# Attention, soft mixture of experts and a softplus layer on one core: q and k in one transfer, w_in in long runs, masks made on the chip

## The chip, the cores and the metric

The kernel runs on one core of one Trainium2 chip. The metric is the time of one execution on the device in microseconds. A second number, the span, is what the hardware profiler records of one execution, from the first to the last thing that it sees; times within the profile count from the start of the span. The core's engines are called PE (TensorE: matmuls and transposes; PEld is its weight load), DVE (VectorE), ACT (ScalarE), POOL (GpSimd) and SP (SyncE, which here only issues transfers). Transfers run on 16 DMA engines that all queues share.

## The reference

Three layers follow one another on 2304 tokens of width 512 (batch 4 x 576 positions; 8 heads of 64). All inputs but w_in and w_out are float32; those two are float64.

```
scores = (q @ k.T) / 8, causal, window of 64;  attn = softmax(scores) @ v     # 4 x 8 x 576 x 64
x      = attn, heads side by side                                            # 2304 x 512
logits = x @ phi                                                             # 2304 x 32 slots
slot_in  = softmax over tokens(logits).T @ x                                 # 32 x 512
slot_out = relu(slot_in[e] @ w1[e]) @ w2[e]      for 8 experts of 4 slots, inner width 1024
x      = softmax over slots(logits) @ slot_out                               # 2304 x 512
out    = softplus(x @ w_in) @ w_out                                          # inner width 2048
```

## The kernel before

**Stage one** (lines 497 to 570) works through 18 tiles of 128 tokens. For a tile, `do_s` multiplies q by the keys of its two blocks of 64 positions (32 small matmuls, L239); `do_t` adds the mask and takes the row maximum on DVE (L250, four operations for each of two halves), `do_m` subtracts the maximum on GpSimd (L257), `do_e` takes the exponential on ACT, `do_pt` transposes on PE with the unit matrix, `do_pv` multiplies by v. The result is normalised, transposed and multiplied by phi; every four tiles a running softmax over tokens is updated. While this goes on, the 32 tiles of w1 (512 KB each) are loaded.

**Stage two** (lines 574 to 749) multiplies the slots by w1 (L594) and w2 (L637). The 32 tiles of w2 are loaded into what stage one and w1 leave free. The first tiles of w_in and w_out are queued before the last two of w2 (lines 732 to 739).

**Stage three** (from line 750) converts w_in and w_out from float64 bit patterns into float32 on DVE (`conv`, L721 to L729, four steps for each half tile), multiplies the slots' output by w_in (`do_wd`, L824, for the first tile), and then computes hidden blocks (`do_h`, L858), softplus on ACT and DVE, and the output products (`do_y`, L887 to L889: three matmuls for each block of 128 x 512, with high and low parts).

**Constants.** One tile `cst_sb` of 128 x 768 floats holds the unit matrix (columns 0 to 127), four masks of 128 columns, of which three are used (128 to 639; the last block is zero), and a selection matrix (640 to 767). It is filled on the host and loaded in one transfer on ACT's queue (L568), behind k of tile 0. A mask has a left and a right half of 64 columns; 0 keeps a score, -8e9 removes it. Mask 1 is for the first tile of a sequence that begins in its upper half, mask 2 for one that begins in the lower half, mask 0 for all others. After stage one, columns 128 to 639 are reused.

**Transfers.** q and k come in tiles of 128 x 512 floats, 2 KB for each partition, v in rows of 2080 bytes. SP issues all of them (k of tile 0 excepted, which ACT issues). There are four buffers each. q of tile t may be loaded when the scores of tile t-4 are done, k when those of t-3 are. A w_in tile is 128 x 4 runs of 1 KB (line 705), a w_out tile 128 runs of 4 KB.

**Order.** Nothing is scheduled at run time. `arrange` simulates the engines with a cost for each step, delays between them and due times, and writes down one order for all engines; each engine then executes its own part of that order and waits at the first instruction whose data isn't there. In stage one, `Q` stands for SP, with costs of 0.67 us for q, k and v and 1.31 us for a w1 tile; `rel` is the earliest start of a step, `FREE_AT` when an engine is free first.

Of the kernel before, what the change touches and what calls it, by code (L numbers as in the profile page):

```python
# [20 lines left out]
FIRST = {0, 9, 18, 27}  # L21
NKB = NQB = NVB = 4
# [15 lines left out]
FREE = dict(E=7.2, A=0.28, D=0.28, P=0.28, Q=0.1)  # L38
FREE_AT = dict(E=3.0, A=4.0, D=3.0, P=3.0, Q=3.6)
L2_END, GOAL, SLACK, NEAR = 7.3, 12.0, 0.65, 0.1  # L40
DELAY = dict(E=0.2, Q=1.0)
LANDS = 2.0
TILE = 4.6
# [5 lines left out]
def arrange(steps, free, ports, tweaks=()):  # L49
# [26 lines left out]
    def make_ready(k):  # L76
        t = steps[k][2]
        for d in steps[k][1]:
            e, end = done[d]
            wait = 0 if e == "Q" and e in steps[k][0] else LANDS if e == "Q" and d[0][0] == "L" else DELAY.get(e, 0.13)  # L80
            t = max(t, end + wait)
        ready[k] = t
# [34 lines left out]
@with_exitstack  # L117
def block_kernel(ctx: ExitStack, tc: tile.TileContext, q, k, v, phi, w1, w2, w_in, w_out, cst, out):
    nc = tc.nc
# [19 lines left out]
    ident = cst_sb[:, 0:128]  # L139
    masks = [cst_sb[:, 128 + 128 * i:256 + 128 * i] for i in range(4)]  # L140
    selr = cst_sb[:, 640:768]
# [50 lines left out]

    kr = sp0.tile([128, NKB, 4, 128], F32, name="kr")
    qb = [sp0.tile([128, 4, 128], F32, name=f"qb{i}") for i in range(NQB)]
    s_acc = sp1.tile([128, DM], F32, name="s_acc")
# [14 lines left out]
    def do_lq(e, t):  # L210
        nc.sync.dma_start(out=qb[t % NQB], in_=q[t])

    def do_lp(e):
        nc.sync.dma_start(out=phi_sb, in_=phi)

    def do_lk(e, t):
        (nc.sync if e == "Q" else nc.scalar).dma_start(out=kr[:, t % NKB], in_=k[t])

# [8 lines left out]
    def do_s(e, t):  # L227
        for a in range(2):
            s_ps[2 * t + a] = bank((2 * t + a) % 3, "s_ps")
        b = t % NKB  # L230
        pb = (t - 1) % NKB if t else b
        for p in range(4):
            for a, par in ((0, 0), (1, 1), (0, 1), (1, 0)):
                rows = slice(64 * a, 64 * a + 64)
                rhs = kr[rows, b, p, :]
                if not par:
                    step = (pb - b) * 512 + 64
                    rhs = bass.AP(tensor=rhs.tensor, offset=rhs.offset, ap=[list(rhs.ap[0]), [step, 2], [1, 64]])
                nc.tensor.matmul(  # L239
                    s_ps[2 * t + a][64 * par:64 * par + 64, 128 * p:128 * p + 128],  # L240
                    qb[t % NQB][rows, p, 64 * par:64 * par + 64], rhs, start=True, stop=True,
                )
# [790 lines left out]
```

## Time and profile before

| | us |
|---|---|
| median of 3 runs | 374.04 (372.24 to 374.28) |
| the profiled execution, its own time | 374.42 |
| its span | 372.6 |
| PE, DVE, ACT, POOL busy | 360.0, 273.5, 232.7, 94.7 |

The granted clock of TensorE is at its full level in every slice. The kernel moves 70.27 MB, 65.02 of it read from HBM. "Busy" counts an engine from an instruction's start to its end; matmuls overlap, so a busy PE can still be waiting in part. The page cuts the span into 40 slices of 9.3 us; the first fourteen are stages one and two.

### The profile page before, as it was taken

To read this page: it belongs to the slowest core of one execution; us is meant where nothing else is said; L and a number is where in the kernel's file an instruction comes from. 1 tells how busy PE (TensorE), PEld (TensorE's weight loads), DVE (VectorE), ACT (ScalarE), POOL (GpSimd) and SP (SyncE) were. 2 spreads that over 40 slices of the span, in tenths; PEclk is the share of its full clock that TensorE was granted. 3 is DMA by queue.
4 is the path that set the end of the run, shared out by engine and by line. 5 is a ranking of instruction groups with operands and counts; after the bars stand their busy time and mean duration, and the time that the engine had idled before them with its cause. 6 is when DMAs were issued, how large, how long until landed. Compare 5 with 4: busy or idle time off the path is not lost.

```text
span 372.6 us, 8160 instructions
## 1 busy us (share of the span) xinstructions
PE 360.0 (97%) x3023; PEld 267.2 (72%) x3023; DVE 273.5 (73%) x780; ACT 232.7 (62%) x458; POOL 94.7 (25%) x113
## 2 busy tenths in 40 slices
PE   8989999999999889999999999999999999999995
PEld 6878778776333256787788778887777787888884
DVE  2776778845440399988998888898998984766653
ACT  2666666674110149889997776878768935556650
POOL 2987777650220001011101320413201000001130
PEclk9999999999999999999999999999999999999999
DMA  8999999999999995135331321330100030200222
GB/s 297 347 355 378 371 392 397 404 407 406 401 406 406 394 370 162 54 97 175 123 103 34 114 91 56 113 113 1 57 2 1 1 114 0 84 30 28 84 87 84
DMA packets 31096, 70.27 MB, mean 189 GB/s; under 512 B 2768, under 2 KB 11088, under 8 KB 31056
## 3 DMA queue, kind: packets, MB, share of 16 engines
q1 hardware_dynamic: 30768, 69.09, 50.8%
q10 hardware_dynamic: 288, 0.66, 0.5%
q8 instruction: 24, 0.39, 0.4%
q14 instruction: 16, 0.13, 0.1%
HBM read 65.02 MB, written 4.72 MB: 187 GB/s over the span
## 4 chain that ended last, share of the span: by engine, by line
PE 82%; DMA 14%; DVE 1%; issue 1%; ACT 1%; POOL 0%; SPq 0%; POOLq 0%
PE y_ps L887 18%; PE y_ps L888 18%; PE y_ps L889 18%; DMA w2t<-w_d 13%; PE s_ps L239 5%; PE x_ps L284 5%; PE pt_ps L266 4%; PE x_ps L858 3%; PE xt_ps L307 2%; PE h_ps L858 2%; DMA kr<-k_d 1%; PE lt_ps L317 1%; PE wq_ps L830 1%; PE warm_ps L152 1%; PE wp_ps L838 1%
## 5 line engine op out<-in xcount | busy, mean ns | idle before, releaser
L887 PE MATMUL y_ps<-whi,gh 128*128 128x512 f32 x288 | 115.2, 400 | 0.0
L888 PE MATMUL y_ps<-wlo,gh 128*128 128x512 f32 x288 | 114.0, 396 | 0.0
L889 PE MATMUL y_ps<-whi,gl 128*128 128x512 f32 x288 | 113.5, 394 | 0.0
L777 POOL TENSOR_TENSOR gl<-g,gh 128x384 fp32r<-128x384 f32 (+1 forms) x27 | 31.5, 1165 | 223.9 <-DVE gh L774 174.8
L887 PEld LDWEIGHTS y_ps<-whi,gh 128*128 128x128 f32 x288 | 54.1, 188 | 14.3 <-issue 1.2
L889 PEld LDWEIGHTS y_ps<-whi,gl 128*128 128x128 f32 x288 | 54.1, 188 | 13.4 <-DVE gl L777 0.3
L888 PEld LDWEIGHTS y_ps<-wlo,gh 128*128 128x128 f32 x288 | 54.1, 188 | 11.2
L866 ACT ACTIVATE a<-a 128x512 f32<-128x512 f32 (+1 forms) x81 | 47.4, 586 | 2.6
L865 ACT ACTIVATE a<-a 128x512 f32<-128x512 f32 (+1 forms) x81 | 47.3, 584 | 1.3
L250 DVE CUSTOM_DVE_ANT_0 sm<-s_ps,cst_sb 128x128 f32<-128x128 f32 x144 | 32.7, 285 | 12.1 <-DMA cst_sb<-cst_d 6.1
L257 POOL TENSOR_TENSOR sm<-mx,sm 128x512 f32<-128x512 f32 x36 | 37.0, 1036 | 16.2 <-DVE mx L250 10.1
L870 DVE SCALAR_TENSOR_TENSOR g<-x_ps,a 128x512 f32<-128x512 f32 (+2 forms) x50 | 31.1, 625 | 12.2 <-ACT a L861 7.0
L861 ACT ACTIVATE a<-x_ps 128x512 f32<-128x512 f32 (+2 forms) x50 | 27.0, 544 | 20.4 <-PE x_ps L858 12.0
L777 DVE TENSOR_TENSOR gl<-g,gh 128x512 fp32r<-128x512 f32 (+2 forms) x54 | 34.4, 639 | 2.3 <-ACT gh L774 0.7
L774 DVE CAST gh<-g 128x512 fp32r<-128x512 f32 (+1 forms) x61 | 24.0, 393 | 11.6 <-PE y_ps L888 11.0
L260 ACT ACTIVATE sm<-sm 128x512 f32<-128x512 f32 x36 | 22.5, 633 | 14.9 <-POOL sm L257 14.4
L861 ACT ACTIVATE a<-h_ps 128x512 f32<-128x512 f32 (+1 forms) x31 | 17.0, 549 | 20.6 <-PE h_ps L858 19.1
L207 ACT COPY pt<-pt_ps 128x512 f32<-128x512 f32 x33 | 18.4, 585 | 9.1 <-PE pt_ps L266 9.0
L284 PE MATMUL x_ps<-vt,pt 128*64 128x65 f32 x288 | 22.0, 226 | 1.6 <-issue 1.5
L284 PEld LDWEIGHTS x_ps<-vd,pt 128*64 128x64 f32 x288 | 18.6, 137 | 6.3 <-issue 5.3
L284 PE MATMUL x_ps<-vd,pt 128*64 128x65 f32 x288 | 22.1, 226 | 0.3 <-POOL vd L275 0.3
L870 DVE SCALAR_TENSOR_TENSOR g<-h_ps,a 128x512 f32<-128x512 f32 (+1 forms) x31 | 19.5, 629 | 3.5 <-ACT a L866 3.2
(141 smaller groups left out, 531.7 us busy)
## 6 DMA issues: line engine op xcount, KB each, us to landing
w1t<-w_d SPq DMA_DIRECT2D x32, 512.0 KB, 7.8
w2t<-w_d SPq DMA_DIRECT2D x29, 512.0 KB, 10.2
wi<-w_in_d SPq DMA_DIRECT2D x16, 512.0 KB, 4.6
wo<-w_out_d SPq DMA_DIRECT2D x16, 512.0 KB, 3.4
vt<-v_d SPq DMA_DIRECT2D x18, 260.0 KB, 6.2
qb<-q_d SPq DMA_DIRECT2D x18, 256.0 KB, 6.3
out_d<-o SPq DMA_DIRECT2D x18, 256.0 KB, 2.0
kr<-k_d SPq DMA_DIRECT2D x17, 256.0 KB, 6.3
```

The lines of the kernel that those rows point to most:

```text
L250: nc.vector.tensor_tensor_reduce(out=sm[:, p], in0=ps[:, 128 * p:128 * p + 128], in1=mask, scale=-0.125, scalar=3.0e38, op0=ALU.add, op1=A ...
L257: nc.gpsimd.tensor_tensor(out=sm_t[i], in0=mb, in1=sm_t[i], op=ALU.subtract)
L284: nc.tensor.matmul(x_ps[64 * par:64 * par + 64, a, 65 * p:65 * p + 65], pt[:, 128 * p + 64 * par:128 * p + 64 * par + 64], vt[:, 65 * h:65 ...
L774: (nc.scalar.copy if e == "A" else nc.vector.tensor_copy)(dst, src)
L777: eng[e].tensor_tensor(out=dst, in0=a, in1=b.bitcast(F32), op=ALU.subtract)
L861: nc.scalar.activation(out=st["a", i], in_=st["h", i], func=AF.Abs)
L865: nc.scalar.activation(out=a, in_=a, func=AF.Exp, scale=-1.0)
L866: nc.scalar.activation(out=a, in_=a, func=AF.Ln, bias=1.0)
L870: nc.vector.scalar_tensor_tensor(out=st["g", i], in0=st["h", i], scalar=0.0, in1=st["a", i], op0=ALU.max, op1=ALU.add)
L887: nc.tensor.matmul(y, st["gh", i][:, ts], hi, start=first, stop=False)
L888: nc.tensor.matmul(y, st["gh", i][:, ts], lo, start=False, stop=False)
L889: nc.tensor.matmul(y, st["gl", i][:, ts], hi, start=False, stop=last)
```

## The change

q and k of a tile become one array in HBM and one transfer of 512 KB, 4 KB for each partition. In SBUF they share the tile `qkb` with four places. For tile 0 the q half is issued by SP and the k half by ACT. The wait of the joint transfer is that of k before: the scores of tile t-3. The planner counts 1.3 us of SP for it, puts loads of q, k and v 1.2 us behind the step that releases their buffer, lets SP be free at 3.1 instead of 3.6 us and scores start at 4.6 instead of 4.8, and drops the earliest start of the mask operation.

w_in is laid out on the host so that each half tile is one block of 128 rows of 4 KB.

The host no longer makes `cst`, and it is not loaded. `make_cst` fills columns with constants on DVE and cuts triangles and the diagonal into them on GpSimd (`affine_select`: keeps an element where base + mult * partition + step * column meets the condition, and writes `fill` elsewhere). The remaining masks and the selection matrix are copies on DVE.

```diff
@@ planner
-FREE_AT = dict(E=3.0, A=4.0, D=3.0, P=3.0, Q=3.6)
+FREE_AT = dict(E=3.0, A=4.0, D=3.0, P=3.0, Q=3.1)
-LANDS = 2.0
+LANDS, LATE = 2.0, 1.2
-            wait = 0 if e == "Q" and e in steps[k][0] else LANDS if e == "Q" and d[0][0] == "L" else DELAY.get(e, 0.13)
+            wait = 0 if e == "Q" and e in steps[k][0] else LANDS if e == "Q" and d[0][0] == "L" else LATE if k[0] in ("LQ", "LV") else DELAY.get(e, 0.13)
@@ constants
+    def make_cst():
+        def keep(x, base, mult, step, op, fill):
+            nc.gpsimd.affine_select(out=x, in_=x, pattern=[[step, x.shape[1]]], base=base, channel_multiplier=mult, compare_op=op, fill=fill)
+
+        l, r = ([m[:, 64 * h:64 * h + 64] for m in masks] for h in range(2))
+        nc.vector.memset(cst_sb[:, 0:512], 0.0)
+        nc.vector.memset(r[1], NONE)
+        keep(l[1], 0, 1, -1, ALU.is_ge, NONE)
+        keep(l[1], 64, -1, 1, ALU.is_gt, NONE)
+        keep(r[1], 63, -1, 1, ALU.is_ge, 0.0)
+        keep(ident, 0, 1, -1, ALU.not_equal, 1.0)
+        keep(r[0], 0, -1, 1, ALU.is_gt, NONE)
+        keep(r[0], 63, -1, 1, ALU.is_ge, 0.0)
+        nc.vector.tensor_copy(l[0], l[1])
+        for i in range(4):
+            p = slice(32 * i, 32 * i + 32)
+            nc.vector.tensor_copy(selr[p].rearrange("p (a c) -> p a c", a=4), ident[p, p].rearrange("p (a c) -> p a c", a=1).to_broadcast([32, 4, 32]))
+        nc.vector.tensor_copy(l[2][0:64], l[1][0:64])
+        nc.vector.memset(l[2][64:128], NONE)
+        nc.vector.tensor_copy(r[2], r[0])
@@ q and k
-    kr = sp0.tile([128, NKB, 4, 128], F32, name="kr")
-    qb = [sp0.tile([128, 4, 128], F32, name=f"qb{i}") for i in range(NQB)]
+    qkb = sp0.tile([128, NKB, 2, 4, 128], F32, name="qkb")
-        nc.sync.dma_start(out=qb[t % NQB], in_=q[t])
+        nc.sync.dma_start(out=qkb[:, t % NKB], in_=qk[t])
-    def do_lk(e, t):
-        (nc.sync if e == "Q" else nc.scalar).dma_start(out=kr[:, t % NKB], in_=k[t])
@@ steps of stage one
-                step_1(("LQ", t), dict(Q=0.67), [("S", t - NQB)])
-                step_1(("LK", t), dict(Q=0.67), [("S", t - NKB + 1)])
+                step_1(("LQ", t), dict(Q=1.3), [("S", t - NKB + 1)])
-            step_1(("S", t), dict(E=1.05), [("LQ", t), ("LK", t), ("LK", t - 1), ("T", 2 * t - 3), ("T", 2 * t - 2)], rel=4.8, goal=5.0 + TILE * t)
+            step_1(("S", t), dict(E=1.05), [("LQ", t), ("T", 2 * t - 3), ("T", 2 * t - 2)], rel=4.6, goal=4.8 + TILE * t)
-                step_1(("T", i), dict(D=0.88), [("S", t), ("PT", i - NSM, last.get(i - NSM)), ("M", i - 4)], rel=6.4)
+                step_1(("T", i), dict(D=0.88), [("S", t), ("PT", i - NSM, last.get(i - NSM)), ("M", i - 4)])
@@ start
-        do_lq("Q", 0)
-        do_lk("A", 0)
-        nc.scalar.dma_start(out=cst_sb, in_=cst)
+        for i, e in enumerate((nc.sync, nc.scalar)):
+            e.dma_start(out=qkb[:, 0, i], in_=qk[0, :, i])
+        make_cst()
         keep_warm(18, 7)
@@ w_in
-                c = 512 * j + 256 * u
-                nc.sync.dma_start(out=t.bitcast(I32).rearrange("p (k f) -> p k f", k=4), in_=w_in[:, c:c + 256].rearrange("(k p) f -> p k f", p=128))
+                src = w_in[2 * j + u]
+            nc.sync.dma_start(out=t.bitcast(I32), in_=src)
```

## Rows read from the trace of the kernel before

**Rows 1.** The page, span in 40 slices: busy tenths of PE and DMA, GB/s moved.

```profile
PE   8989999999999889999999999999999999999995
DMA  8999999999999995135331321330100030200222
GB/s 297 347 355 378 371 392 397 404 407 406 401 406 406 394 370 162 54 97 175 123 103 34 114 91 56 113 113 1 57 2 1 1 114 0 84 30 28 84 87 84
```

**Rows 2.** Chain that ended last, in order of time: start us, us, what.

```profile
83.73 10.13 DMA w2t<-w_d
...
121.76 10.41 DMA w2t<-w_d
```

**Rows 3.** Windows: length, busy us (count) of PE PEld DVE ACT POOL, clock, DMA, GB/s.

```profile
8.00:12.00 4.00, 4.00 (x76) 3.17 (x70) 2.84 (x27) 2.36 (x5) 3.88 (x6) 1.00 1.05 391
...
16.00:20.00 4.00, 4.00 (x86) 3.44 (x79) 2.96 (x20) 2.61 (x5) 3.82 (x6) 1.00 0.96 284
20.00:24.00 4.00, 2.45 (x44) 2.08 (x42) 2.14 (x12) 1.36 (x4) 3.21 (x4) 1.00 0.96 335
...
84.00:88.00 4.00, 3.68 (x81) 3.17 (x79) 2.00 (x8) 2.27 (x8) 0.00 (x0) 1.00 1.02 405
...
112.00:116.00 4.00, 3.55 (x32) 1.53 (x25) 0.58 (x4) 0.00 (x0) 0.00 (x0) 1.00 1.03 410
...
132.00:136.00 4.00, 3.65 (x24) 2.28 (x25) 3.83 (x7) 1.72 (x5) 0.00 (x0) 1.00 1.07 370
136.00:140.00 4.00, 3.62 (x30) 2.98 (x29) 3.60 (x10) 2.84 (x10) 0.00 (x0) 1.00 1.01 357
```

**Rows 4.** DMA queues: packets; issues with count, KB each, median us to landing.

```profile
DMA packets 31096, 70.27 MB, mean 189 GB/s; under 512 B 2768, under 2 KB 11088, under 8 KB 31056
...
w2t<-w_d SPq DMA_DIRECT2D x29, 512.0 KB, 10.2
...
kr<-k_d SPq DMA_DIRECT2D x17, 256.0 KB, 6.3
...
cst_sb<-cst_d ACTq DMA_DIRECT2D x1, 384.0 KB, 4.8
```

**Rows 5.** Waits of SP's queue: engine, line, waited for: us, times, longest.

```profile
SPq L168 <- DMA w2t<-w_d: 20.1, 25, 1.6
...
SPq L217 <- PE s_ps L239: 7.8, 11, 1.4
...
SPq L168 <- PE ld_ps L317: 0.9, 1, 0.9
```

**Rows 6.** Timeline at the seam: start, us, engine line op, tiles, [idle before <-releaser].

```profile
130.91 1.05 PE L637 MATMUL l_ps<-w2t,hTz 128*32 128x512 f32 x4 [2.29 <-DMA w2t<-w_d]
...
141.67 0.39 PE L887 MATMUL y_ps<-whi,gh 128*128 128x512 f32 x1
...
125.44 0.69 DVE L749 CAST cT<-c_ps 128x512 fp32r<-128x512 f32 x1 [2.47 <-PE c_ps L748]
128.33 0.43 DVE L723 TENSOR_SCALAR cv<-wi 128x512 f32<-128x512 f32 x1 [2.20 <-DMA wi<-w_in_d]
```

**Rows 7.** Groups of POOL by shape: busy us, mean ns | idle before, releasers.

```profile
L777 POOL TENSOR_TENSOR gl<-g,gh 128x512 fp32r<-128x512 f32 x10 | 14.1, 1414 | 98.5 <-DVE gh L774 77.4 <-PE h_ps L858 9.3 <-PE wp_ps L838 7.8
...
L672 POOL TENSOR_TENSOR cc<-lnat,cc 128x128 fp32r<-128x128 f32 x4 | 1.8, 484 | 2.4 <-ACT cc L670 2.4
L672 POOL TENSOR_TENSOR cc<-lnat,cc 128x64 fp32r<-128x64 f32 x1 | 0.4, 363 | 0.0
```

**Rows 8.** Timeline at the start.

```profile
0.73 0.20 POOL L565 MEMSET ones<- 128x128 f32 x1 [0.29 <-POOLq L1021]
...
4.59 1.10 PE L239 MATMUL s_ps<-kr,qb 64*64 64x128 f32 x32
...
6.15 0.29 DVE L250 CUSTOM_DVE_ANT_0 sm<-s_ps,cst_sb 128x128 f32<-128x128 f32 x1 [6.15 <-DMA cst_sb<-cst_d]
...
6.79 1.53 PE L239 MATMUL s_ps<-kr,qb 64*64 64x128 f32 x32 [0.45 <-DMA kr<-k_d]
```

More of the change, by code (lines that the diff above doesn't have):

```diff
@@ L21 @@
 FIRST = {0, 9, 18, 27}
-NKB = NQB = NVB = 4
+NKB = NVB = 4
 NSM, NPT = 5, 3
@@ L27 @@
 NX = 9
+NONE = -8.0e9
 NA, NG, NH = 4, 2, 3
@@ L117, in block_kernel @@
 @with_exitstack
-def block_kernel(ctx: ExitStack, tc: tile.TileContext, q, k, v, phi, w1, w2, w_in, w_out, cst, out):
+def block_kernel(ctx: ExitStack, tc: tile.TileContext, qk, v, phi, w1, w2, w_in, w_out, out):
     nc = tc.nc
@@ L139, in block_kernel @@
     ident = cst_sb[:, 0:128]
-    masks = [cst_sb[:, 128 + 128 * i:256 + 128 * i] for i in range(4)]
+    masks = [cst_sb[:, 128 + 128 * i:256 + 128 * i] for i in range(3)]
     selr = cst_sb[:, 640:768]
@@ L234, in do_s @@
                 rows = slice(64 * a, 64 * a + 64)
-                rhs = kr[rows, b, p, :]
+                rhs = qkb[rows, b, 1, p, :]
                 if not par:
-                    step = (pb - b) * 512 + 64
+                    step = (pb - b) * 1024 + 64
                     rhs = bass.AP(tensor=rhs.tensor, offset=rhs.offset, ap=[list(rhs.ap[0]), [step, 2], [1, 64]])
@@ L240, in do_s @@
                     s_ps[2 * t + a][64 * par:64 * par + 64, 128 * p:128 * p + 128],
-                    qb[t % NQB][rows, p, 64 * par:64 * par + 64], rhs, start=True, stop=True,
+                    qkb[rows, b, 0, p, 64 * par:64 * par + 64], rhs, start=True, stop=True,
                 )
@@ L475, in emit_rinv @@
         nc.vector.reciprocal(r, r)
-    do_1 = dict(LP=do_lp, LQ=do_lq, LK=do_lk, LV=do_lv, LW=do_w1, S=do_s, T=do_t, M=do_m, E=do_e, PT=do_pt, PC=do_pc, VD=do_vd, PV=do_pv,
+    do_1 = dict(LP=do_lp, LQ=do_lq, LV=do_lv, LW=do_w1, S=do_s, T=do_t, M=do_m, E=do_e, PT=do_pt, PC=do_pc, VD=do_vd, PV=do_pv,
                 RI=do_ri, XN=do_xn, XT=do_xt, XC=do_xc, LG=do_lg, LT=do_lt, DM=do_dm, DE=do_de, DT=do_dt, DN=do_dn, SL=do_sl,
@@ L703, in load_raw @@
             if kind == "wi":
-                c = 512 * j + 256 * u
-                nc.sync.dma_start(out=t.bitcast(I32).rearrange("p (k f) -> p k f", k=4), in_=w_in[:, c:c + 256].rearrange("(k p) f -> p k f", p=128))
+                src = w_in[2 * j + u]
             else:
                 r = 256 * j + 128 * u
-                nc.sync.dma_start(out=t.bitcast(I32), in_=w_out[r:r + 128, :])
+                src = w_out[r:r + 128, :]
+            nc.sync.dma_start(out=t.bitcast(I32), in_=src)
         def conv(dst, src):
@@ L1003 @@
     vh[:, :, 0:64] = v.transpose(0, 2, 1, 3).reshape(NTOK, 8, 64)
-    cst = np.zeros((128, 768), np.float32)
-    cst[:, 0:128] = np.eye(128)
-    qi = (np.arange(128) % 64)[:, None]
-    j = np.arange(64)[None, :]
-    own = np.where(j <= qi, 0.0, -8.0e9)
-    prev = np.where(j > qi, 0.0, -8.0e9)
-    none = np.full((128, 64), -8.0e9)
-    even = {x: np.concatenate((own, x_prev), 1)[0:64] for x, x_prev in ((0, prev), (1, none))}
-    odd = {x: np.concatenate((x_prev, own), 1)[64:128] for x, x_prev in ((0, prev), (1, none))}
-    for i, (x, y) in enumerate([(0, 0), (1, 0), (0, 1)]):
-        cst[:, 128 + 128 * i:256 + 128 * i] = np.concatenate((even[x], odd[y]))
-    cst[:, 640:768] = (np.arange(128)[:, None] % 32 == np.arange(128)[None, :] % 32)
     ins = [
-        ("q_d", pairs(q)), ("k_d", pairs(k)), ("v_d", vh.reshape(NTOK, 520)), ("phi_d", inputs["moe_phi"].reshape(4, 128, NS).transpose(1, 0, 2)),
+        ("qk_d", np.stack((pairs(q), pairs(k)), 2)), ("v_d", vh.reshape(NTOK, 520)), ("phi_d", inputs["moe_phi"].reshape(4, 128, NS).transpose(1, 0, 2)),
         ("w1_d", inputs["moe_w1"]), ("w2_d", inputs["moe_w2"]),
-        ("w_in_d", bits(inputs["moe2_w_in"])), ("w_out_d", bits(inputs["moe2_w_out"])), ("cst_d", cst),
+        ("w_in_d", bits(inputs["moe2_w_in"]).reshape(4, 128, 16, 128).transpose(2, 1, 0, 3).reshape(16, 128, 512)), ("w_out_d", bits(inputs["moe2_w_out"])),
     ]
```

## The prediction

> **What bounds the kernel now.** The page's slices come first [rows 1]: in the first fourteen slices (130 us) the DMA line reads 8 to 9 tenths and the GB/s line runs from 297 to 407, while PE reads 8 to 9; from the sixteenth slice on DMA drops and PE stays at 9. So the span has two halves: a loading half in which both DMA and PE look full, and a half that only PE fills. The chain of waits says which of the two ends the first half [rows 2]: from 83.73 to 132.17 us it is a string of transfers of w2, each released by the one before it, and only then matmuls (L637). In the windows of the first half [rows 3] the DMA share is above 1, with the exception of 16 to 24 us (0.96): transfers follow one another without a gap, and the last w2 tile lands when everything queued ahead of it has been moved. That the queue is deep is seen in the issues and in the waits of the issuing engine [rows 4, 5]: a w2 tile of 512 KB takes 1.28 us at 408 GB/s but lands 10.2 us after its issue, so some eight are queued, and SP waits 20.1 us for older w2 transfers but only 0.9 us for PE.
>
> At the seam between the halves [rows 6] PE stands still 2.29 us before the last-but-one w2 tile, and DVE 2.20 us before the first tile of w_in: its conversion starts at 128.33, behind a copy that ends at 126.13. Both wait for the same queue. Behind 128.33 DVE converts one tile after the other in the written order, and the first y matmul, at 141.67, needs the second w_in tile too. From there PE is full to the end [rows 1], with its y matmuls in a fixed order. So what the load queue gains at the seam, up to the point where PE or DVE stop waiting for it, comes off the end one for one; what PE alone gains in the first half does not.
>
> **The change part by part.** The profiled execution took 374.42 us (span 372.6, so 1.8 around it), 0.38 above the median of 374.04. The sum is made against 374.42 and its difference put on the median.
>
> *cst is not loaded.* It is one transfer of 384 KB [rows 4], 393,216 bytes; at 408 GB/s, the mean of the windows with nothing but 4 KB runs (405 and 410, [rows 3]), 0.96 us less in a queue that has no gap. Where the queue has a gap the gain is nothing, and only the windows of 16 to 24 us show one.
>
> *q and k in one transfer.* No byte less, but 2,304 runs of 4 KB for 4,608 of 2 KB (18 tiles of 128 partitions, each with 512 floats of q and as many of k). What a run costs beyond its bytes has no row of its own; it comes out of rates [rows 3]. At 408 GB/s a 4 KB run takes 160.6 ns on each of 16 engines. From 8 to 12 us only q, k and v move, at 391 GB/s. One partition row of the three is 6,176 bytes, and I count it as four runs, since v's rows of 2,080 bytes leave a short packet (of the 2,768 packets under 512 B [rows 4], 2,304 are one for each row of v). It takes 6,176 x 16 / 391 = 252.7 ns; with o for each run, 252.7 = 4 o + 1.508 (160.6 - o), so o = 4.2 ns. From the other side, 132 to 136 us: w_in and w_out tiles alternate at 370 GB/s, 1.417 us a tile in the mean; w_out with 4 KB runs is 1.285, so w_in with four times the runs is 1.55, 0.26 more, and 0.26 x 16 / (3 x 128) gives o = 11 ns. The first is measured on q and k themselves, but counts v's short packet in full; I take 7 ns, between them: 2,304 x 7 / 16 = 1.0 us less, with the ends 0.6 and 1.6. The 18 issues that go are SP's, which is not the bound.
>
> *w_in in 4 KB runs.* One w_in tile lies ahead of the last two w2 tiles in the queue, so 0.26 us comes off (0.1 if o is 4.2 ns, 0.37 at the 357 GB/s of the next window). The other fifteen lie behind the seam, where no conversion but the first waited for its data: they give nothing.
>
> The Trainium skill (DMA: Bandwidth & Descriptors, Why small descriptors are slow) gives the engine's internal bus a fixed 3 cycles a packet beside one cycle for each 32 bytes. By that q and k would give 2.2% of their 23 us, about 0.5 us, and the w_in tile 0.09, and the sum would be 1.6 instead of 2.2; the rates in the rows show a larger price for a run, and I stay with them.
>
> *Masks, unit and selection matrix made on the chip.* DVE fills 512 columns (a DVE pass over 512 floats is 0.43 us, [rows 6]) and 64 more from 0.73 us, when the engines start, to about 1.3. GpSimd then makes six selections, five of 64 columns and one of 128. No row shows a selection. From below: its memset of 128 columns, 0.20 us [rows 8], six times 1.2 us. From above: a GpSimd subtraction of 512 columns, 1.414 us [rows 7], six times 8.5 us. Nearest in size are the two-input rows of 64 and 128 columns, 363 and 484 ns: 5 x 0.36 + 0.48 = 2.3 us, which I take. DVE's eight small copies and fills run beside them except the last two or three, which I put at 0.4 us. So all is ready at about 4.0 us (2.9 to 10.2). All of it stands in DVE's program before the first mask operation and in GpSimd's before its first subtraction, and behind these wait ACT's exponentials and PE's transposes.
>
> Now that first operation starts at 6.15 us, after 6.15 us of waiting for cst [rows 8], though the scores were ready at about 5.7 (32 matmuls from 4.59, 1.10 us). With masks at 4.0 it starts at about 5.8, 0.35 us earlier; the scores of tile 1, which waited for k until 6.79, come about 1 us earlier, because 384 KB no longer shares the engines with them. This shifts stage one by some 0.35 us, which by itself is worth nothing: at the seam PE waits. It moves DVE's copy, now ending at 126.13, by the same.
>
> *The order on the queues.* q of tile t now waits for the scores of t-3, as k did, and no longer for t-4. k waits at that point 7.8 us over 11 issues [rows 5]. At 4.6 us a tile (the planner's own figure) the data has 13.8 us to arrive; it lands in 6.3 [rows 4]. The planner also puts the loads of q, k and v 1.2 us behind their release, so w1 tiles go ahead of them and SP stands less behind a wait. What the new order does to PE I can't read from the trace; a loss up to the 2.2 us by which PE and DVE wait at the seam is covered, and beyond that it counts in full.
>
> **Sum.** 0.96 + 1.0 + 0.26 = 2.2 us off the queue (1.7 to 2.9). DVE's wait of 2.20, less 0.05 behind the copy, is the lid: what is late next is that copy, unless stage one moves too. I take 2.15: 374.42 - 2.15 = 372.27, and on the median 371.9 us.
>
> **Rivals.** *Only the bytes count* (373.1): a run costs nothing beside its bytes, or a rearranged stage one leaves DVE and PE less to gain at the seam; then cst's 0.96 is all. For it: the DMA share is no lower in windows of 2 KB runs, and 391 against 408 could be v's short packets alone. Against: 370 GB/s where 1 KB runs move.
>
> *The queue's dip goes too* (370.0): between 16 and 24 us it moves 284 and 335 GB/s, 8 us x (1 - 309.5 / 408) = 1.9 us lost. If w1 tiles issued earlier fill it, and stage one moves along (PE was busy 2.45 of 4 us from 20 to 24), both add: 374.04 - 2.15 - 1.9 = 370.0. Against: phi's 64 KB in short runs is loaded there as before, and the share is 0.96, so little of it is a gap.
>
> *The masks come too late* (375.9, the other side): GpSimd is slow at the selections, the first mask operation moves behind 6.15 and all of stage one with it, since DVE and GpSimd hold their queues in order. It decides from the point at which the delay exceeds 2.2 us, first mask operation at 8.3. At 1.41 us each: 1.3 + 8.5 + 0.4 = 10.2 us, 4.05 late, 1.85 above the lid, 374.04 + 1.85 = 375.9. For it: no selection is in the trace. Against: GpSimd's two-input work of this size takes a third of that.
>
> The Trainium skill (GPSIMD Engine Reference, Instruction dispatch) puts about 6 us, without a row in the profile, on the first call of a freshly loaded kernel. If a selection is such a call, the masks come at about 10 us and this rival's time is the result; no run here shows it yet.
>
> **How the numbers follow.** Forecast 0.46, only the bytes 0.25, the dip too 0.16, late masks 0.13. What a measurement can tell from no change is 0.5%, 1.87 us: the border is 372.17, and the forecast with its own spread (a gain of 1.7 to 2.5, the lid with stage one's 0.35) lies beyond it in seven cases of ten. Faster 0.7 x 0.46 + 0.16 = 0.48, same 0.14 + 0.25 = 0.39, slower 0.13. The range reaches from the dip's 370.0 to 374.5, where a start 2.6 us late would put it.
>
> **What would show it.** Right: no cst transfer; about 405 GB/s where q, k and v move; last w2 tile landed near 129.9; DVE's wait before the first conversion gone or below 0.3 us; first mask operation near 5.8; first y matmul near 139.5; everything behind it shifted alike. Selections over 0.5 us each or a first mask operation later than 8.3 show the late masks; a last w2 landing near 131.2 shows that runs cost nothing. The forecast is wrong at its base if the load queue has gaps in the new order, or if PE no longer waits for w2 at the seam.

## The result and the profile after

| us | before | after |
|---|---|---|
| median | 374.04 (5 runs, 372.24 to 374.5) | 370.67 (5 runs, 370.36 to 371.76) |
| ratio, with its 95% interval | | 0.9912 (0.9884 to 0.994) |
| the profiled execution | 374.42 | 370.36 |
| its span | 372.6 | 368.6 |

The change is 3.4 us faster by the medians. Repeated later (a_again, below) it was 0.9932 (0.9908 to 0.9955), 2.6 us. The profiled executions differ by 4.06 us, but the one of before lies in the upper part of its own runs, so a part of these 4.06 is not the change's.

The slices of the span after, as in [rows 1]: the load queue has one weak place left (slice 2, 333 GB/s) and then stays above 400 to the tenth slice, where before it needed seven slices to get to 397 and more.

```profile
PE   8999999998999999999999999999999999999995
DMA  7999999999999993115421311330000030200222
GB/s 300 333 409 404 402 404 403 404 409 408 381 403 408 410 366 126 59 57 172 133 96 57 115 60 58 115 116 24 33 2 2 1 114 0 90 25 28 86 87 85
```

The chain that ended last (start, us, what), as in [rows 2]: one transfer of w2 is left in it, and what stands ahead of it is the work of stages one and two (113.58 is a w2 matmul). Before, the chain at this place was a string of transfers from 83.73 on.

```profile
113.58 4.34 PE l_ps L659 x37
...
117.92 10.17 DMA w2t<-w_d
...
128.13 1.05 PE l_ps L659 x4
```

Windows after, as in [rows 3]. In place of the old dip at 16 to 24 us (284 and 335 GB/s) there is one at 8 to 16 us.

```profile
8.00:12.00 4.00, 4.00 (x79) 3.35 (x81) 3.15 (x29) 2.59 (x5) 3.88 (x5) 1.00 0.95 325
12.00:16.00 4.00, 3.61 (x91) 2.99 (x84) 3.40 (x26) 2.80 (x6) 3.81 (x6) 1.00 0.97 338
16.00:20.00 4.00, 4.00 (x80) 3.45 (x78) 2.89 (x18) 2.38 (x5) 3.82 (x6) 1.00 1.00 387
20.00:24.00 4.00, 4.00 (x101) 3.57 (x102) 3.70 (x25) 2.72 (x5) 3.88 (x6) 1.00 1.03 410
...
24.00:40.00 16.00, 15.97 (x310) 12.82 (x309) 10.99 (x70) 11.95 (x26) 13.61 (x17) 1.00 1.03 403
```

Two more windows of before, which the prediction had not looked at: 24 to 40 us, and 36 to 40 within it. The third line, from b_mid below, is the order of before in a second execution (its edit comes at 73 us).

```profile
24.00:40.00 16.00, 15.94 (x325) 12.63 (x325) 11.57 (x77) 11.96 (x26) 13.14 (x16) 1.00 1.02 371
...
36.00:40.00 4.00, 4.00 (x68) 2.48 (x68) 2.90 (x19) 3.61 (x9) 3.31 (x4) 1.00 1.00 345
```

```profile
24.00:40.00 16.00, 15.28 (x310) 12.01 (x304) 10.65 (x72) 11.23 (x25) 12.72 (x16) 1.00 0.99 363
```

The last column is what to compare, not the one before it. At a DMA share of 0.99 to 1.02 before's order moved 345 to 371 GB/s, the new one 403 at 1.03: a share near 1 does not show that the queue moves all it can.

Nor was the queue empty in that stretch. Each of the 18 transfers that before issued from 24 to 40 us landed 5.3 to 7.5 us later, though 512 KB take 1.28 us at 408 GB/s, so some 2 MB stood queued all the while. The packets themselves took longer: those of 2 KB 99 to 118 ns in the mean from 37 to 40 us, where 84 is their median from 40 to 72 us. What slowed them no run shows. The page of before gives the median landing of a w1 tile:

```profile
w1t<-w_d SPq DMA_DIRECT2D x32, 512.0 KB, 7.8
```

SP's waits after (us in all, times, longest): for buffers of q and k 16.5 us, for those of v 21.2, where before it was 7.8 for k [rows 5] and 11.7 for v. So it isn't that SP waits less; what differs is the order in which it issues.

```profile
SPq L244 <- PE x_ps L307: 21.2, 14, 2.9
...
SPq L237 <- PE s_ps L262: 16.5, 13, 3.8
```

The queue's packets and issues, as in [rows 4]: 0.39 MB less, and no cst.

```profile
DMA packets 22360, 69.88 MB, mean 190 GB/s; under 512 B 2480, under 2 KB 2608, under 8 KB 22320
...
qkb<-qk_d SPq DMA_DIRECT2D x17, 512.0 KB, 6.9
```

The seam (start, us, engine, idle before), as in [rows 6]. PE's wait for w2 went from 2.29 to 0.29 us, DVE's for w_in from 2.20 to 0.28; DVE's copy is 2.06 us earlier and the first y matmul 4.08.

```profile
126.85 1.05 PE L659 MATMUL l_ps<-w2t,hTz 128*32 128x512 f32 x4 [0.29 <-DMA w2t<-w_d]
128.13 1.05 PE L659 MATMUL l_ps<-w2t,hTz 128*32 128x512 f32 x4 [0.23 <-DMA w2t<-w_d]
...
137.59 0.40 PE L909 MATMUL y_ps<-whi,gh 128*128 128x512 f32 x1
...
123.38 0.69 DVE L771 CAST cT<-c_ps 128x512 fp32r<-128x512 f32 x1 [2.47 <-PE c_ps L770]
124.34 0.43 DVE L745 TENSOR_SCALAR cv<-wi 128x512 f32<-128x512 f32 x1 [0.28 <-DMA wi<-w_in_d]
```

The last four w2 matmuls of before, to which the second line above compares:

```profile
132.21 1.05 PE L637 MATMUL l_ps<-w2t,hTz 128*32 128x512 f32 x4 [0.25 <-DMA w2t<-w_d]
```

The start, as in [rows 8]: GpSimd's six selections, DVE's last copy for the masks (3.93 + 0.20 = 4.13 us), the scores and the first mask operation, which now waits for the scores; then the selections by shape (busy us, mean ns).

```profile
1.54 1.47 POOL L140 TENSOR_SCALAR_AFFINE_SELECT cst_sb<-cst_sb 128x64 f32<-128x64 f32 x6 [0.54 <-DVE cst_sb L143]
3.93 0.20 DVE L157 COPY cst_sb<-cst_sb 128x64 f32<-128x64 f32 x1
4.68 1.10 PE L262 MATMUL s_ps<-qkb 64*64 64x128 f32 x32
5.84 0.29 DVE L273 CUSTOM_DVE_ANT_0 sm<-s_ps,cst_sb 128x128 f32<-128x128 f32 x1 [1.71 <-PE s_ps L262]
```

```profile
L140 POOL TENSOR_SCALAR_AFFINE_SELECT cst_sb<-cst_sb 128x64 f32<-128x64 f32 x5 | 1.1, 238 | 0.7 <-DVE cst_sb L143 0.5
L140 POOL TENSOR_SCALAR_AFFINE_SELECT cst_sb<-cst_sb 128x128 f32<-128x128 f32 x1 | 0.3, 292 | 0.0
```

PE's operations come in the same order in both kernels. DVE, ACT and POOL differ only by the constants and q's and k's transfers; on SP the loads of q, k, v, w1 and phi come in another order.

### The profile page after: what moved, and what is told of

Same layout as the page of the kernel before. It is cut to its first block, busy times and chain, and to the rows that moved or that the text cites. A ratio compares the mean times of both kernels' runs of the same rounds, so it can differ in the third digit from the quotient of the medians.

```text
span 368.6 us, 8153 instructions
## 1 busy us (share of the span) xinstructions
PE 359.5 (98%) x3023; PEld 267.0 (72%) x3023; DVE 275.6 (75%) x790; ACT 232.5 (63%) x458; POOL 96.0 (26%) x119
## 2 busy tenths in 40 slices
DMA packets 22360, 69.88 MB, mean 190 GB/s; under 512 B 2480, under 2 KB 2608, under 8 KB 22320
## 4 chain that ended last, share of the span: by engine, by line
PE 89%; DVE 3%; DMA 3%; POOL 2%; issue 1%; ACT 1%; DVEq 0%; POOLq 0%
PE y_ps L909 18%; PE y_ps L910 18%; PE y_ps L911 18%; PE x_ps L307 5%; PE s_ps L262 4%; PE pt_ps L289 4%; PE l_ps L616 4%; PE x_ps L880 3%; DMA w2t<-w_d 3%; PE xt_ps L330 2%; PE l_ps L659 2%; PE h_ps L880 2%; POOL sm L280 1%; PE warm_ps L179 1%; PE lt_ps L340 1%; PE wq_ps L852 1%
```

## The experiments

They ran in three groups, each beside before on one chip; a ratio is to before of the same group (medians 374.36, 373.12 and 373.68). "T" below is the planner's name of the mask step.

### Numbers that all runs share

"Rest" is the time of the profiled execution less the start of its first y matmul. "Last w2" is the start of the last four w2 matmuls, "copy" that of DVE's last copy at the seam (the CAST into cT above), which tells how late stage one's chain is. "Moved" is what the load queue had moved by 72 us, without cst: 24 us x the rate of 0 to 24 us, plus 48 us x that of 24 to 72, less 0.39 MB where cst is loaded; "ahead" is the difference from before at 408 GB/s. Behind the table stand the two windows of before and of after.

| | time | first y | rest | last w2 | copy | moved, MB | ahead, us |
|---|---|---|---|---|---|---|---|
| before | 374.42 | 141.67 | 232.75 | 132.21 | 125.44 | 25.98 | 0 |
| b_chip | 372.60 | 139.85 | 232.75 | 130.40 | 125.02 | 26.62 | 1.6 |
| b_plan | 371.82 | 139.06 | 232.76 | 129.59 | 124.09 | 26.87 | 2.2 |
| b_mid | 374.50 | 141.61 | 232.89 | 132.14 | 126.13 | 26.03 | 0.1 |
| b_delay | 379.04 | 146.29 | 232.75 | 136.83 | 131.16 | 23.73 | -5.5 |
| a_oldplan | 372.21 | 139.42 | 232.79 | 129.96 | 124.00 | 26.93 | 2.3 |
| a_2kb | 372.50 | 139.74 | 232.76 | 130.28 | 125.24 | 26.78 | 2.0 |
| a_w1first | 372.56 | 139.68 | 232.88 | 130.23 | 125.82 | 26.78 | 2.0 |
| a_win1k | 371.18 | 138.41 | 232.77 | 128.94 | 123.79 | 27.38 | 3.4 |
| after | 370.36 | 137.59 | 232.77 | 128.13 | 123.38 | 27.46 | 3.6 |
| a_again | 370.59 | 137.81 | 232.78 | 128.35 | 124.24 | 27.22 | 3.0 |
| a_cst | 372.91 | 139.98 | 232.93 | 130.47 | 126.41 | 26.58 | 1.5 |
| a_mid | 371.38 | 138.62 | 232.76 | 128.47 | 125.04 | 27.41 | 3.5 |
| a_delay | 376.70 | 143.96 | 232.74 | 133.84 | 130.38 | 24.96 | -2.5 |

```profile
0.00:24.00 24.00, 20.97 (x359) 16.72 (x359) 13.11 (x98) 10.41 (x18) 15.97 (x24) 1.00 0.93 323
24.00:72.00 48.00, 47.94 (x962) 38.31 (x961) 38.19 (x226) 31.17 (x67) 36.88 (x46) 1.00 1.03 388
```

```profile
0.00:24.00 24.00, 22.43 (x419) 18.23 (x421) 17.18 (x121) 11.85 (x20) 18.27 (x32) 1.00 0.91 338
24.00:72.00 48.00, 47.98 (x946) 38.24 (x941) 38.05 (x225) 31.11 (x67) 36.90 (x46) 1.00 1.03 403
```

Whatever happens ahead of the first y matmul, 232.74 to 232.93 us follow: each run is decided at the seam. And there, within 0.02 us in all fourteen, the first y matmul starts at the later of two times: 9.46 us behind "last w2", or 13.58 us behind "copy". The load queue (last w2) decides in ten of them, stage one (copy) in a_cst, a_mid and a_delay; in a_again both give the same.

The time also goes with the queue's lead: in the nine rows of kernels without fills, before apart, the profiled execution is shorter than before's by 1.5 to 4.1 us, each within about 0.8 us of what the queue is ahead. That alone does not show which is the cause, since SP waits for buffers that PE frees, so that a late stage one holds back the queue too. All these are single executions. Before's runs go from 372.2 to 375.3 us in the second group alone, so the gains by medians, given below, are smaller.

### The parts taken back one at a time

**a_2kb**: q and k again in runs of 2 KB, all issues as in the changed kernel.

```diff
-        nc.sync.dma_start(out=qkb[:, t % NKB], in_=qk[t])
+        nc.sync.dma_start(out=qkb[:, t % NKB], in_=qk[t].rearrange("c p a b -> p c a b"))
...
-        ("qk_d", np.stack((pairs(q), pairs(k)), 2))
+        ("qk_d", np.stack((pairs(q), pairs(k)), 1))
```

> The changed kernel, with one edit: q and k of a tile lie one behind the other in HBM, so the joint transfer moves two runs of 2 KB for each partition instead of one of 4 KB. Issues, order and bytes stay. Changed kernel: 370.7 us, last w2 tile landed at 128.1 in its profile. Theory 'runs' (the load queue ends the first half and a run costs 7 ns beside its bytes, as predicted): 2,304 x 7 / 16 = 1.0 us later at the seam, 371.7. Theory 'runs cost more' (the 1.9 us that the seam moved beyond the predicted 2.2 are run costs that I put too low): +2.5 to 2.9, 373.4. Theory 'order' (the rest came from SP's new order): +1.0 or less; theory 'bytes only': 0, 370.7.

Measured: 371.77 us, ratio 0.9925 (0.99 to 0.995); the intervals of this and of the changed kernel overlap, so the time decides nothing. The rate and the packets tell more. The window of 40 to 72 us, a_2kb first and a_again, the unchanged kernel, behind it:

```profile
40.00:72.00 32.00, 32.00 (x635) 25.68 (x630) 26.59 (x149) 18.91 (x42) 23.71 (x30) 1.00 1.03 397
```

```profile
40.00:72.00 32.00, 32.00 (x649) 25.59 (x651) 27.19 (x153) 19.37 (x43) 23.77 (x30) 1.00 1.03 404
```

397 against 404 is 0.55 us of 32, in which some seven tiles of q and k move (32 / 4.6), each with 128 runs more over 16 engines: 56 o = 0.55, o = 9.8 ns for a run. One pair of executions would not carry this, for in the same window a_mid, a_delay, a_cst and a_w1first move 400, 397, 395 and 391 with 4 KB runs; but their DMA share is 1.01 to 1.02. At a share of 1.03 or more the runs part: 403 to 405 GB/s in the four with 4 KB runs (after, a_again, a_win1k, a_oldplan), 389 to 399 in the six with 2 KB runs (a_2kb, before and the four runs built on it). By 72 us a_2kb is 1.1 us behind a_again (26.78 against 27.22 MB), but so is a_w1first with 4 KB runs.

The trace's own packets give the price directly. From 40 to 72 us a packet of 2 KB takes 84 or 85 ns in the median and one of 4 KB 161 or 162, in every run that has them; one of 1 KB (w_in before, over the whole span) takes 46. Two of 2 KB take 6 to 9 ns longer than one of 4 KB, and two of 1 KB 7 or 8 ns longer than one of 2 KB. The prediction took 7 ns for a run and 1.0 us for all.

**a_win1k**: w_in again in runs of 1 KB.

```diff
-                src = w_in[2 * j + u]
+                nc.sync.dma_start(out=t.bitcast(I32).rearrange("p (k f) -> p k f", k=4), in_=w_in[:, c:c + 256].rearrange("(k p) f -> p k f", p=128))
```

> The changed kernel with w_in loaded in 1 KB runs as before; all else stays. Theory 'runs': one w_in tile lies ahead of the last w2 tiles, 0.26 us, 370.9; the other fifteen cost nothing. If w_in's runs matter in the third stage too (conversions waiting for them), +1 us or more and waits of DVE on w_in in the profile. 'Bytes only': 370.7.

Measured: 370.95 us, 0.9903 (0.9865 to 0.994): no loss in the time that could be told. At the seam PE waits 0.67 and DVE 0.69 us, 0.4 more than in the changed kernel, and 104 to 128 us move 402 GB/s where the changed kernel moves 409 in both its executions (24 us x 7 / 409 = 0.41 us). The term was forecast at 0.26; it exists, and it is below what the time can show.

```profile
104.00:128.00 24.00, 22.51 (x184) 7.91 (x186) 6.37 (x19) 2.23 (x4) 0.00 (x0) 1.00 1.03 402
```

**a_cst**: the constants loaded again.

```diff
-        make_cst()
+        nc.scalar.dma_start(out=cst_sb, in_=cst)
```

> The changed kernel with the constants loaded from HBM on ACT's queue behind k of tile 0, as before, and nothing made on the chip. Theory 'queue': 0.96 us more at the seam, 371.6 to 371.7, first mask operation again near 6.1 us. If stage one decides at the seam: its start moves by 0.3 us only, 371.0.

Measured: 372.22 us, 0.994 (0.9913 to 0.9967), by the ratios 1.0 and 0.3 us more than the changed kernel in its two measurements, with intervals that overlap. Nor does the one execution show the way that the forecast names. The first mask operation starts at 7.20, 12 to 16 us move 275 GB/s (338 and 330 in the two executions of the changed kernel), and no w2 matmul waits at the seam: the last 24 stand in one piece. Stage one ends last here, but only by 0.06 us, for last w2 is 2.3 us later than in after, too. How much of this the load of cst makes is not shown, since a_again, without it, starts slowly as well (below).

```profile
7.20 0.29 DVE L273 CUSTOM_DVE_ANT_0 sm<-s_ps,cst_sb 128x128 f32<-128x128 f32 x1 [7.20 <-PE warm_ps L179]
...
127.67 3.86 PE L659 MATMUL l_ps<-w2t,hTz 128*32 128x512 f32 x24
```

**a_oldplan**: the transfers of the changed kernel with the planner's numbers of before. These are the parts that the prediction had priced, and the joint transfer's own place in SP's order.

```diff
-FREE_AT = dict(E=3.0, A=4.0, D=3.0, P=3.0, Q=3.1)
+FREE_AT = dict(E=3.0, A=4.0, D=3.0, P=3.0, Q=3.6)
...
-            wait = ... else LATE if k[0] in ("LQ", "LV") else DELAY.get(e, 0.13)
+            wait = ... else DELAY.get(e, 0.13)
...
-rel=4.6, goal=4.8 + TILE * t
+rel=4.8, goal=5.0 + TILE * t
```

(the mask step also has its `rel=6.4` back)

> The changed kernel with the planner's four numbers set back (no 1.2 us behind a release for loads of q, k and v, SP free at 3.6, scores from 4.8, mask operation from 6.4). PE, DVE, ACT and GpSimd keep the same order; only SP's differs, by where v, q and k and w1 stand to one another. Theory 'order': the surplus of some 1.2 to 1.9 us over the predicted gain goes, 372 to 372.5. Theories 'runs' and 'queue': the same bytes in the same runs, 370.7 within 0.3.

Measured: 371.69 us, 0.9932 (0.9906 to 0.9957), 2.7 us faster than before by the medians, between the times of the two theories. From 24 to 40 us it moves 378 GB/s (403 after, 371 before), and PE waits 1.50 us for w2 again.

```profile
24.00:40.00 16.00, 15.66 (x298) 12.51 (x298) 10.69 (x67) 11.61 (x25) 13.29 (x17) 1.00 1.02 378
```

```profile
128.68 1.05 PE L659 MATMUL l_ps<-w2t,hTz 128*32 128x512 f32 x4 [1.50 <-DMA w2t<-w_d]
```

### The parts done alone on the kernel before

**b_plan**: only the planner's numbers, so only SP's order; every transfer as before.

```diff
-FREE_AT = dict(E=3.0, A=4.0, D=3.0, P=3.0, Q=3.6)
+FREE_AT = dict(E=3.0, A=4.0, D=3.0, P=3.0, Q=3.1)
...
+            wait = ... else LATE if k[0] in ("LQ", "LK", "LV") else DELAY.get(e, 0.13)
```

(with rel=4.6 and no `rel` at the mask step)

> The kernel before with the planner's four numbers of the changed kernel alone (its 1.2 us also for k); transfers, runs and constants as before. Only SP's order differs. Theory 'order' (in the kernel before SP stood ahead of waits with too little queued, 350 and 345 GB/s in the windows from 28 and 36 us, and the new order lets w1 go ahead): 1.0 us less at the seam, 373.4 where before is 374.4. Theory 'runs and bytes only': 0.

Measured: 371.72 us, 0.9958 (0.9939 to 0.9976), 1.4 us faster by the medians with not a byte less. 16 to 20 us, third line, went from 284 to 388 GB/s, and PE's wait at the seam from 2.29 to 1.02 us. phi, in the same short runs, is issued at 9.9 us here and at 14.4 before; no window from 8 to 24 us falls below 386.

```profile
8.00:12.00 4.00, 4.00 (x80) 3.24 (x80) 2.77 (x25) 1.76 (x3) 3.88 (x5) 1.00 1.05 390
12.00:16.00 4.00, 4.00 (x92) 3.52 (x95) 3.40 (x31) 2.71 (x5) 3.88 (x6) 1.00 1.06 386
16.00:20.00 4.00, 3.75 (x95) 3.13 (x87) 3.49 (x21) 2.61 (x6) 3.81 (x6) 1.00 1.04 388
20.00:24.00 4.00, 4.00 (x84) 3.58 (x80) 3.36 (x21) 3.03 (x7) 3.84 (x5) 1.00 1.03 394
```

```profile
128.29 1.05 PE L637 MATMUL l_ps<-w2t,hTz 128*32 128x512 f32 x4 [1.02 <-DMA w2t<-w_d]
```

**b_chip**: only the constants made on the chip.

```diff
-        nc.scalar.dma_start(out=cst_sb, in_=cst)
+        make_cst()
```

> The kernel before with the constants made on the chip and not loaded; transfers of q, k, v and w_in and the order as before. Theory 'queue': 0.96 us less, 373.4. If the gain of the chip-made constants is in the start of stage one and not in the bytes: 0 here, since stage one has room at the seam, 374.4.

Measured: 372.72 us, 0.9993 (0.9975 to 1.0012): a gain of at most 0.9 us, just short of the 0.96 that were forecast, and none that can be told from nothing. Its profiled execution is 1.6 us ahead in bytes and 1.8 us shorter than that of before, but the median of before in this group is lower than that execution by 1.3 us. The order's weak stretch stands as in before, now from 12 to 20 us:

```profile
12.00:16.00 4.00, 3.69 (x88) 3.04 (x86) 3.40 (x26) 2.79 (x6) 3.81 (x6) 1.00 1.01 340
16.00:20.00 4.00, 3.92 (x79) 3.54 (x80) 2.90 (x20) 2.60 (x5) 3.82 (x6) 1.00 0.96 317
```

### How late may the masks be?

**b_delay** and **a_delay**: fills of another tile on DVE ahead of the first mask operation.

```diff
+        for _ in range(15):   # 8 in a_delay
+            nc.vector.memset(s_acc, 0.0)
         keep_warm(18, 7)
```

> The kernel before with fifteen DVE fills of 128 x 512 (0.48 us each in the changed kernel's profile) of a buffer that is written later anyway, put ahead of the first mask operation, so that it starts at about 8.2 us instead of 6.15. Theory 'lid' (before the change stage one has 2.2 us to spare at the seam, where PE and DVE wait for the load queue): no change within 0.3 us, and DVE's wait before the first w_in conversion shrinks from 2.20 to about 0.2. Theory 'stage one decides': +2.0 us.

> The changed kernel with eight such fills, so that the first mask operation starts at about 8.0 instead of 5.84 us, 2.1 us late. Theory 'lid': the changed kernel has only about 0.3 us to spare at the seam (PE 0.29 and DVE 0.28 us of waiting in its profile), so +1.8 us, some 372.9. Theory 'queue alone': 0, 371.1. So the same delay is free in the one kernel and costs nearly its whole length in the other, if the lid holds.

Measured: b_delay 379.45 us, 1.0174 (1.014 to 1.0209); a_delay 376.18 us, 1.007 (1.004 to 1.01). The fills took longer than planned, 0.66 us each with the wait between two of them, so the first mask operation of b_delay started at 10.53 (4.4 late) and that of a_delay at 9.19 (3.4 late). Even so, by the prediction's rule (delay less the waiting at the seam, 2.2 and 0.3 us) they should have lost 2.2 and about 3. b_delay lost 6.3 us; a_delay lost some 5 to 5.5 us against the medians of the changed kernel, which did not run in this group. The trace of b_delay shows by what way. PE waits 4.07 us for the score banks that the mask operations free, SP waits 5.7 us for those scores ahead of the next load of k, with w1 queued behind it, and from 12 to 14 us nothing at all is moved; the granted clock (the third figure from the end: 0.92, 0.50, 0.73) falls to its lower level of 1.2 GHz, at which 30 score matmuls take 1.91 us where 32 took 1.10 [rows 8]. a_delay shows the same: SP waits 7.9 us, 8 GB/s from 10 to 12 us, a granted clock of 0.50 from 10 to 16.

```profile
11.55 1.91 PE L239 MATMUL s_ps<-kr,qb 64*64 64x128 f32 x30 [4.07 <-DVE mx L250]
```

```profile
SPq L217 <- PE s_ps L239: 9.7, 5, 5.7
```

```profile
10.00:12.00 2.00, 0.45 (x12) 0.48 (x16) 1.87 (x16) 0.00 (x0) 0.52 (x1) 0.92 0.82 303
12.00:14.00 2.00, 2.00 (x29) 1.48 (x23) 0.76 (x9) 1.08 (x2) 1.94 (x3) 0.50 0.00 0
14.00:16.00 2.00, 2.00 (x24) 1.56 (x26) 1.26 (x12) 0.46 (x2) 1.94 (x4) 0.73 0.68 200
```

At the seam PE of b_delay still waits for w2, 1.20 us: it is the queue that ends last. In a_delay stage one does, by 0.7 us (table).

```profile
135.54 1.05 PE L639 MATMUL l_ps<-w2t,hTz 128*32 128x512 f32 x4 [1.20 <-DMA w2t<-w_d]
```

So a delay at the start does not stay in stage one, where the slack would swallow it: it passes to the load queue. How the loss divides between the queue's gap and the lower clock was not tested.

### A delay that does not reach the queue

**b_mid** and **a_mid**: six small fills on DVE at mask step 34, behind the last loads of q and k.

```diff
+        if i == 34:
+            for _ in range(6):
+                nc.vector.memset(cst_sb[:, 512:640], 0.0)
```

> The kernel before with six DVE fills of 128 x 128 (about 0.34 us each with the wait that the fills of the longer delay showed) ahead of the mask operation of the last tile of stage one, near 74 us. There the queue holds only w1 and w2, and SP stands ahead of nothing that these fills hold up for long, so stage one alone is late, by about 2.0 us. Theory 'lid' (2.2 us of waiting at the seam): 0 to +0.3 us, DVE's wait before the first w_in conversion down from 2.20 to about 0.2. If stage one decides: +2.0.

> The changed kernel with the same six fills at the same place, 2.0 us late. Theory 'lid' (0.3 us of waiting at the seam): +1.7 us. If the load queue alone decides there: 0.

Measured: the fills took 1.46 us in place of the 2.0 planned. b_mid 374.11 us, 1.0013 (0.9992 to 1.0034); a_mid 371.79 us, 0.9948 (0.9925 to 0.9972), 0.7 above a_again. The times of the two don't tell the theories apart. The profiles do, with the table's two paths. In b_mid the copy is 0.69 us later than in before (126.13), PE and DVE wait some 0.75 us less for w2 and w_in, the queue still ends last, and the span is 372.7 (372.6 before). In a_mid the copy is 0.80 us later than in a_again (125.04) and the span 0.8 longer (369.7 against 368.9). Against the other execution of the changed kernel the copy is 1.66 us later and the first y 1.03, since stage one had 0.63 us to spare there. The delays of the copy differ from the 1.46 us of the fills because the bases start at different times (a_again below). The line is PE's wait of b_mid at the seam; a_mid has none.

```profile
130.86 1.05 PE L640 MATMUL l_ps<-w2t,hTz 128*32 128x512 f32 x4 [1.54 <-DMA w2t<-w_d]
```

### The gap that is left, and the kernel again

**a_w1first**: the first w1 tile issued ahead of q and k of tile 4, against the gap at 8 to 16 us.

```diff
-        for _, e, key in arrange(steps_1, FREE_AT, {}):
+        order_1 = arrange(steps_1, FREE_AT, {})
+        keys = [x[2] for x in order_1]
+        w1_first = order_1.pop(keys.index(("LW", 0)))
+        keys = [x[2] for x in order_1]
+        order_1.insert(keys.index(("LQ", 4)), w1_first)
+        for _, e, key in order_1:
```

> The changed kernel with the first w1 tile issued ahead of q and k of tile 4, where SP stands 3.8 us for the scores of tile 1 and the queue runs low (share 0.8 from 10 to 13 us). Theory 'the order leaves a gap there': the windows from 8 to 16 us rise from 325 and 338 GB/s towards 400, and the queue is about 1 us earlier at the seam; stage one isn't, so by the lid only some 0.3 us is to be had, 370.4. If stage one waits for loads in that stretch too, up to 1 us. If the later q and k of tile 4 hold PE up: slower.

Measured: 371.78 us, 0.9951 (0.9931 to 0.997): no gain. The gap moved behind the extra tile (306 and 330 GB/s in a_again), 8 to 12 us at 407 GB/s and 12 to 16 at 296.

```profile
8.00:12.00 4.00, 4.00 (x82) 3.24 (x76) 2.77 (x27) 1.80 (x4) 3.88 (x5) 1.00 1.02 407
12.00:16.00 4.00, 4.00 (x100) 3.52 (x102) 3.40 (x33) 2.79 (x6) 3.88 (x6) 1.00 0.92 296
```

**a_again**: the changed kernel without an edit.

> The changed kernel unchanged, on the same chip as the three others, so that they have a direct neighbour: 0.991 of before, some 370.7 us.

Measured: 371.11 us, 0.9932 (0.9908 to 0.9955). In this execution the first mask operation starts at 6.66 (5.84 in the other), because the 18 warm-up matmuls ahead of it took 4.02 us in place of 3.69 and the 32 of the scores 1.58 in place of 1.10, at a granted clock of 1.00 in both. No matmul or conversion at the seam waits for the queue: by the table both paths give 137.81 or 137.82, while in the other execution the queue ended last by 0.63 us. So stage one and the load queue now end nearly together, and which of them ends last changes from one execution to the next. No kernel that ran was faster than this one by more than the intervals allow.

## Why the prediction came out right, and where it did not

*The bound and its place: right for the kernel before.* The load queue ended the first half, and what last w2 gained came off the end one for one, 4.08 us at the seam and 4.06 in the time. The table shows it to 0.2 us in fourteen executions. DVE's wait for w_in, which the prediction set beside PE's, did not decide: the first y follows last w2.

*The sum of 2.2 us: supported, in the sum more than in its terms.* a_oldplan is nearest to what was summed. It is 2.3 us ahead by 72 us, its last w2 is 2.25 us earlier than before's (129.96; the prediction has the last w2 tile land near 129.9), and it gained 2.7 us by the medians (1.6 to 3.5). Of the terms, the runs of q and k were forecast at 1.0 us, at 7 ns a run, and the packets show 6 to 9 ns; the w_in tile at 0.26, and 0.4 show at the seam; cst at 0.96, which taken alone (b_chip) could not be told from nothing. The times of the runs resolve none of the three.

*The first working of o was wrong.* It counted a short packet for each row of v. After, there are 2480 packets under 512 B with the same rows of v, 288 fewer for 18 fewer transfers; 2768 = 16 x 173 and 2480 = 16 x 155. They are 16 for each transfer, not v's. With three runs a row, 252.7 = 3 o + 1.508 (160.6 - o) gives 7.0 ns and not 4.2. The value chosen was near the packets' 6 to 9; one of its two bounds was not a bound.

*The step that failed: "The order on the queues".* It says that w1 tiles go ahead and SP stands less behind a wait, and then enters the order with no gain. b_plan shows that SP's order alone was worth 1.4 us (0.9 to 2.3) on the kernel before. With the priced parts in place it shows less: a_oldplan, without it, gained 2.7 us, the changed kernel 3.4 and 2.6, with intervals that overlap, though by 72 us the queue of the changed kernel is 1.3 and 0.7 us further ahead. The measured 370.67 lies 1.2 us below the forecast of 371.9. Only a rival, at a chance of 0.16, had a gain of the order in it; how much of the 1.2 us it makes the times don't tell. That the result still fell inside the range is in part luck: the range's lower end, 370.0, is that rival's price and not the forecast's.

The premise behind it was a misreading: "transfers follow one another without a gap", from a share near 1. The prediction saw the dip at 16 to 24 us and held against its going that phi's short runs lie there and that the share is 0.96. b_plan loads phi in the same runs 4.5 us earlier and moves 386 to 394 GB/s all the way from 8 to 24 us, so the low 284 GB/s, which b_mid repeats (286), came with the order. Nor did the prediction look at 24 to 40 us, where before lost (1 - 371 / 403) x 16 = 1.3 us at a share of 1.02. b_plan gets 382 there and a_oldplan 378, but b_chip, with before's order and runs, 395: what this stretch is short of can't be put down to the order and the longer runs alone. By what way the order gains stays open. SP does not wait less, and before's queue was not empty in its weak windows. Nor was the lateness of 1.2 us tried apart from the planner's other numbers.

Two of the prediction's own signs came out against it: where q, k and v move, 8 to 16 us, the rate is 325 and 338 GB/s in place of about 405, and in a_again PE no longer waits for w2 at the seam. It had named gaps in the new order and the end of that wait as what would show its base wrong. The base held all the same in the first execution, where the queue ends last by 0.63 us, and the queue's gain elsewhere outweighs the gap.

*The lid of 2.15: mis-sized.* By the table's two paths stage one had 2.65 us to spare in before (141.67 against 125.44 + 13.58), and the order moved stage one as well, which was put at 0.35 us: DVE's copy came 2.06 us earlier in after, and 1.35 in b_plan. The parts don't add up: 2.7 us (a_oldplan) and 1.4 (b_plan) by the medians, and 2.6 and 3.4 for both. That there is a lid is shown: a_mid lengthens the span by what it delays stage one beyond the slack. How much of the 4.06 us between the two profiles is the change and how much before's own spread is open.

*Of the rivals,* the outcome lies between the forecast (371.9) and "the queue's dip goes too" (370.0). The dip moved more than it went: from 8 to 24 us the mean is 345 GB/s in before and 360 in b_mid, 365 in after and 350 in a_again. Of the 3.6 and 3.0 us that the two executions of the changed kernel are ahead at 72 us, 1.8 came behind 24 us, and 0.96 of the remainder is cst. "Only the bytes count" (373.1) is refuted by the packets' times and by both measurements of the time. "The masks come too late" did not happen: the selections took 238 and 292 ns each, the masks were ready at 4.13 us (4.0 forecast), the first mask operation started at 5.84 (5.8 forecast). But its price was wrong. It was worked out as the delay less 2.2 us of slack, and the two delays show that a late start costs more than the delay itself, through the score banks and the load queue, and with a lower clock.

The Trainium skill (DMA: Bandwidth & Descriptors, Why small descriptors are slow) would give 3.7 ns a run by its 3 cycles a packet, an estimate from that page at 160.6 ns for 131 cycles; the packets of this case put it at 6 to 9 ns, about twice that, and the measurement decides. The Trainium skill (GPSIMD Engine Reference, Instruction dispatch) names about 6 us for a freshly loaded kernel's first call; here six selections were done 3.01 us after the span's start, so no wait of that length lay ahead of them within the span.

Open: why the warm-up and score matmuls of one and the same kernel take longer in one execution than in another at the same granted clock, by what way the order of the issues raises the rate, and what each of the three priced terms is worth in time by itself.

## What to carry to other kernels

Where one queue of transfers ends a stage, look at its GB/s window by window against the best window of the same kernel; a busy share near 1 can hide a rate a tenth or more below it. An engine that issues in order and waits for a free buffer holds up everything behind the wait, and when the wait is long enough, as in the two delays, the queue runs empty. The order of the issues can be worth as much as the bytes. Ask which of two paths ends last at a seam, and by how much, before pricing either. And a slack at the end of a stage covers a delay only as long as the delay doesn't hold back the loads themselves.

## What the runs showed of the hardware

- Each transfer left 16 packets under 512 B in the count (2768 for 173 transfers, 2480 for 155).
- From 40 to 72 us, at a DMA share of 1.03 or more, the kernels with 4 KB runs of q and k moved 403 to 405 GB/s, those with 2 KB runs 389 to 399.
- A packet of 1, 2 and 4 KB took 46, 84 to 85 and 161 to 162 ns in the median: some 7 ns beside its bytes.
- With transfers queued all the while (5.3 to 7.5 us from issue to landing) and a DMA share of 1.02, before moved 371 GB/s from 24 to 40 us, where the changed kernel moved 403.
- GpSimd's selection of 128 x 64 floats takes 238 ns, of 128 x 128 floats 292 ns, less than its two-input work of that width (363 and 484 ns, [rows 7]).
- In b_delay, behind 4 us in which PE was busy for 0.45 (8 to 12 us), its clock was granted at 0.50 (1.2 GHz) from 12 to 14 us; 30 score matmuls took 1.91 us where 32 took 1.10 at the full level.
